# Idle matmuls from the first microseconds, the parameter rows spread at another place, and one batch's attention moved six steps ahead

## The chip, the cores and the metric

The kernel runs on one core of a Trainium2 chip. A core has five engines that work side by side, each through its own instructions in order: TensorE (PE) multiplies matrices into PSUM, VectorE (DVE), ScalarE (ACT) and GpSimd (POOL) work on elements, and SyncE (SP) mostly starts DMA transfers. They wait for each other through semaphores. The metric is the time of one execution on the device in microseconds, and the figure quoted is the median of several runs.

## The reference

Sliding-window attention with sink tokens is followed by a mixer block; each of the four batches is independent, only the parameters are shared.

```python
# q, k, v: (4, 8, 768, 64); n_sink = 4; window = 128
scores = scale * np.matmul(q, k.transpose(0, 1, 3, 2))
keep = (pos[None, :] < n_sink) | ((rel >= 0) & (rel < window))   # rel = query - key
a = softmax(np.where(keep, scores, -1e9))
x = np.matmul(a, v)                        # -> (4, 768, 512): heads side by side

a1 = alpha1 * x + beta1
u = x + lam * np.einsum('ts,bsd->btd', w_tok, a1)      # mixes the 768 tokens
a2 = alpha2 * u + beta2
out = u + lam * (np.maximum(a2 @ w_ch1, 0.0) @ w_ch2)  # 512 -> 2048 -> 512
```

Inputs and the output are float32; the kernel multiplies in fp16.

## The kernel before

Per batch, q and k are loaded, cast to fp16 (`n`, L317 and L315) and transposed into `qkT`: on TensorE for batches 0 and 1 (`tp`, L521), by DMA for batches 2 and 3 (L534). The 768 rows are six blocks of 128. For each key block j, `scores` (L607, L612) multiplies it with the queries of its own and the next block, which is all that the window reaches. ScalarE takes the exponential into `E` (L627). In batch 0, TensorE adds the mask before the exponential (L607); in later batches VectorE multiplies it in afterwards (L636). The sink keys have a small product of their own (`sk`, L560, with key slices `ks`, and `es`, L565). `pv` (L652, L659) multiplies with v, and VectorE divides by the sum (L682, L683). Batch 0 is done in two halves of four heads (G = 0, 1), so that its first half can start before all of q and k is there.

GpSimd then makes `xh` (L692, L701, L704): x times lam*alpha1, and plus lam*beta1 (in batch 0 this part is added in the token product instead, by a seventh matmul with the row sums of w_tok, L790; `lb` and `rsr` serve for it). `tok` (L786) is the token product, six output blocks per batch with six matmuls each; VectorE adds it to x (L795), which gives u. u is cast (`u16`), transposed to `uT` (on TensorE in batch 0, L830; by DMA later, L848) and scaled by alpha2, beta2 (L813, L815). `mlp1` (L869) makes 16 blocks of `h` for each of two chunks of three row blocks, with the relu on ScalarE or VectorE (L875, L877). `mlp2` (L893) multiplies with w2, which VectorE or GpSimd has multiplied with lam on its way to fp16 (`w2f`, L768), in four parts for each of six row blocks. VectorE adds (L904), and SyncE stores (L907).

The parameters come as rows. lam, alpha1 and beta1 are single rows of 512 elements. GpSimd multiplies two of them with lam (L938, L940). `spread` (L759) then copies a row to all 128 partitions by a float32 matmul of a column of ones with it: `b_la` for lam*alpha1, `b_lb1b` for lam*beta1, `b_lam` for lam. VectorE or ScalarE copies the result to `la_b`, `lb_b` and `lam_b`. alpha2 and beta2 are transposed into columns (`abT`, L949).

PSUM has eight banks. Four are homes of kind "d", taken by everything that TensorE makes except the scores; two homes of two banks each, kind "S", are for the scores.

The order of all this isn't written out. Every step is a task with a priority, costs in nanoseconds for each engine that may do it, the tasks that it follows and the buffers that it uses. `Plan.emit` runs a model of the engines and DMA rings once, when the program is made. It repeatedly picks the task that can start earliest (by priority among equals), gives it the engine and a home for its buffers, and writes its instruction at the end of that engine's queue. A change in one planned time can therefore reorder everything that follows, and even choose another engine for a step. On the chip, each engine goes through its queue in that order and waits as its data demands.

Where the model sees TensorE without work ahead of a task, up to 36 us of planned time (`IDLE`), it puts in idle matmuls: 128x128 products of the identity `iden` into a free home of kind "d" (L308) whose result nobody reads. Their number is the planned gap divided by 75 ns, counted from 900 ns at the earliest. The model counts TensorE's costs twice for tasks that start before 4500 ns.

Later batches are laid over earlier ones: while batch b is in mlp1 and mlp2, attention of batch b + 1 is spread over the same steps. Each batch's MLP is a list of steps with priorities w0, w0 + 1, and so on; the attention steps of the next batch get priorities that run evenly from w0 + lo to w0 + hi. For batch 1, lo is `LO`; for batches 2 and 3 it is 1. SyncE's queue holds loads, DMA transposes and stores in planned order; GpSimd's has casts, products and the issue of four loads of w1 (L480).

Of the kernel before, what the change touches and what calls it, by code (L numbers as in the profile page):

```python
# [15 lines left out]
PE, ACT, DVE, POOL, SP = "pe", "act", "dve", "pool", "sp"  # L16
# [91 lines left out]
class Plan:  # L108
# [10 lines left out]
    def add(self, prio, engs, fn, after=(), uses=(), mode=None, lands=None, port=False,  # L119
            since=0.0):  # L120


        t = Task(prio, engs, fn, after, uses, mode, lands, port)
        t.ready = max(t.ready, since)
        for b in uses:
            b.left += 1
        for a in t.needs:
            a.then.append(t)
        self.tasks.append(t)
        return t  # L130

    def emit(self):
        order = sorted(range(len(self.tasks)), key=lambda i: (self.tasks[i].prio, i))
        rank = {id(self.tasks[i]): r for r, i in enumerate(order)}
        waiting = {id(t): len(t.needs) for t in self.tasks}
        open_ = []
        free = {e: 0.0 for e in (PE, ACT, DVE, POOL, SP)}
        rings = Rings()

        def admit(t):  # L140
            bisect.insort(open_, (rank[id(t)], t), key=lambda x: x[0])

        def end(t, seen):
            t.seen = seen
            for b in t.uses:
                b.left -= 1
                b.freed = max(b.freed, seen)
                if b.left == 0:
                    self.busy[b.kind][b.home] = False
                    self.homes[b.kind][b.home] = b.freed  # L150
            for o in t.then:
                o.ready = max(o.ready, seen)
                waiting[id(o)] -= 1
                if not waiting[id(o)]:
                    admit(o)

        def pick():
            best = None
            for r, t in open_:
                at = t.ready  # L160
                for b in t.uses:
                    if b.t is None and b.home is None:
                        homes = [h for h, x in zip(self.homes[b.kind], self.busy[b.kind]) if not x]
                        n = sum(1 for o in t.uses if o.t is None and o.kind == b.kind)
                        if len(homes) < n:
                            at = None
                            break
                        at = max(at, sorted(homes)[n - 1])
                if at is None:
                    continue  # L170
                for e in t.engs:
                    at_e = max(free[e], at)
                    if e == POOL or (e == DVE and t.port):
                        at_e = max(at_e, port)
                    key = (at_e, r, at_e + t.engs[e])
                    if best is None or key < best[0]:
                        best = (key, t, e)
            return best

        for t in self.tasks:  # L180
            if not waiting[id(t)]:
                admit(t)
        mode = None
        port = 0.0
        landing = float("inf")
        done = 0
        while done < len(self.tasks):
            best = pick()
            if best is None or landing <= best[0][0]:
                assert landing < float("inf"), "no task can go on"  # L190
                t = rings.step(float("inf"))
                end(t, rings.now + 300.0)
                landing = rings.peek()
                continue
            (start, r, _), t, e = best
            open_.remove((r, t))
            for b in t.uses:
                if b.t is None:
                    spare = [i for i, x in enumerate(self.busy[b.kind]) if not x]
                    b.home = min(spare, key=lambda i: self.homes[b.kind][i])  # L200
                    self.busy[b.kind][b.home] = True
                    pool, shape, dtype = self.pools[b.kind]
                    b.t = pool.tile(b.shape or shape, b.dtype or dtype,
                                    tag=f"{b.kind}_{b.home}", bufs=1, name=b.name)
            until, idle, took = self.fill
            n = int((start - max(free[PE], 900.0)) / took)
            if e == PE and free[PE] < until and n > 0:
                free_d = [(h, i) for i, (h, x) in enumerate(zip(self.homes["d"], self.busy["d"])) if not x]
                if free_d and min(free_d)[0] < free[PE]:
                    h = min(free_d)[1]  # L210
                    idle(self.pools["d"][0].tile(
                        [P_, 512], FP32, tag=f"d_{h}", bufs=1, name=f"idle{done}"), n)
                    self.homes["d"][h] = start
                    mode = None
            t.fn(e)
            cost = t.engs[e]
            if t.lands:
                cost += rings.room("sw" if e == POOL else "hw", t.lands, start) - start
            if e == PE:
                if start < 4500.0:  # L220
                    cost = cost * 2
                if t.mode != mode:
                    cost = cost + 95
                mode = t.mode
            free[e] = start + cost
            if e == POOL or (e == DVE and t.port):
                port = free[e]
            t.at = (e, start, free[e])
            done += 1
            if t.lands:  # L230
                rings.step(start)
                rings.issue("sw" if e == POOL else "hw", t, free[e])
                landing = rings.peek()
            else:
                end(t, free[e] + SEEN[e])
        self.ends = free
# [3 lines left out]
def kernel(  # L240
# [72 lines left out]
    def copy(e, o, i):  # L313
        if e == ACT:
            nc.scalar.copy(o, i)  # L315
        else:
            engine[e].tensor_copy(o, i)  # L317
# [88 lines left out]
    w1f = const.tile([P, NC, DFF], FP16, name="w1f")  # L406
    w2f = const.tile([P, NF, DM], FP16, name="w2f")

    ROWS = 5500.0
    SPREAD = -790  # L410
    W1_SINCE = 20000.0

# [23 lines left out]
    def load_v(p, b, r, wait=None):  # L436
        bf = vn[b, r] = Buf("vnat", None, None, f"vnat{b}_{r}")
        done["vn", b, r] = add(
            p, {SP: 550}, lambda e: nc.sync.dma_start(
                bf.t, v[b, :, r * P : (r + 1) * P, :].rearrange("h p d -> p h d")),  # L440
            [wait], [bf], lands=(64, 19.0))
# [314 lines left out]
    def spread(p, name, src, o):  # L756

        pt = Buf("d", None, None, f"b_{name}")
        a = add(p, {PE: 900}, lambda e: nc.tensor.matmul(pt.t, ones_r, src, start=True, stop=True),  # L759
                [done.get(name)], [pt], since=ROWS)  # L760
        done[name] = add(p + 0.1, {DVE: 600, ACT: 600}, lambda e: copy(e, o, pt.t), [a], [pt])
# [153 lines left out]
    n = 0  # L915
# [21 lines left out]
    def spread_rows():  # L937
        done["la1"] = add(-880, {POOL: 1270}, lambda e: nc.gpsimd.tensor_mul(rows[1], rows[1], rows[0]),  # L938
                          since=ROWS)
        a = done["lb1b"] = add(-878, {POOL: 1270}, lambda e: nc.gpsimd.tensor_mul(rows[2], rows[2], rows[0]),  # L940
                               since=ROWS)
        z = add(-990, {POOL: 400}, lambda e: nc.gpsimd.memset(lb16.t, 0.0), [], [lb16])
# [6 lines left out]
        a = add(-850, {PE: 200}, lambda e: nc.tensor.transpose(pt.t, ab_row, iden8), [], [pt],  # L949
                since=ROWS)  # L950
        done["ab2"] = add(-800, {DVE: 100, ACT: 230}, lambda e: copy(e, ab2, pt.t), [a], [pt])
# [21 lines left out]


    STEP = 100.0
    LO = 12
    LEAD = 46.0
    for b in range(B):
        w0 = STEP * b
# [30 lines left out]
        if b + 1 < B:  # L1010
            nb = b + 1
            if nb >= XB:
                for i, (hp, t) in enumerate(QK_ORDER):
                    load_qk(w0 + i, nb, hp, t, done["qkT", b, 3, 1])
                for r in range(NR):
                    load_v(w0 + 10 + r, nb, r, done["qkT", b, 3, 1])
            lo, hi = (1, ns - 14) if b else (LO, ns - 12)
            steps = [("T", i) for i in range(8)] + [("sk",)]
# [58 lines left out]
```

## Time and profile before

| what | before |
|---|---|
| median of 6 runs | 272.58 us (271.46 to 274.88) |
| the profiled execution | 271.86 us, span 270.2 us |
| TensorE busy | 257.2 us, 95% of the span, 1844 matmuls |
| VectorE, ScalarE, GpSimd busy | 144.4, 134.8 and 109.5 us |
| HBM read and written | 29.63 and 6.29 MB |
| token products L786 | 34.5 us, 144 matmuls |
| mlp1 L869 | 90.2 us, 512 matmuls |
| mlp2 L893 | 89.0 us, 384 matmuls |

The span runs from the first to the last instruction of the program; what lies around it belongs to the execution's time too. [...] matmuls are pipelined, so the distance between two starts says how fast TensorE goes, not the length of one. In a line of the timeline, the bracket tells how long the engine was idle before it, and what ended that.

### The profile page before, as it was taken

The page shows a single profiled execution, that of the slowest core. Times are in us where ns is not written, and L with a number is a line of the kernel's source. Part 1 is how long each engine was busy: PE and PEld are TensorE (multiplying, and loading weights), DVE is VectorE, ACT ScalarE, POOL GpSimd, SP SyncE. Part 2 cuts the span into 40 slices and gives each one's busy share as a digit, 9 for nine tenths or more (in the row PEclk, how much of TensorE's full clock was granted, in tenths as well). Part 3 has the DMA queues.
Part 4 walks back from the last instruction along what each step waited for, and adds up shares of the span by engine and source line. Part 5 has one row for each costly group of instructions (what it writes and reads, how often), then busy time and mean ns, then how long its engine had stood idle before and what let it go on. Part 6 is the DMA issues. An engine that isn't in the chain of part 4 may idle for free.

```text
span 270.2 us, 4769 instructions
## 1 busy us (share of the span) xinstructions
PE 257.2 (95%) x1844; PEld 137.5 (51%) x1844; DVE 144.4 (53%) x299; ACT 134.8 (50%) x222; POOL 109.5 (41%) x124
## 2 busy tenths in 40 slices
PE   3899989998999999799999999999999999999994
PEld 2344555764554554356555444555654445665441
DVE  4267665579798755727894235378952344000222
ACT  3359983766756224878870024787600136773000
POOL 8544893667492672035595223005755000000000
PEclk9999999999999999999999999999999999999999
DMA  6999999929953999499919897200011252000222
GB/s 208 335 230 367 379 295 247 164 80 271 268 86 82 227 238 212 107 245 229 183 31 143 181 232 175 61 0 2 0 41 40 97 98 79 0 0 2 79 78 78
DMA packets 85484, 39.64 MB, mean 147 GB/s; under 512 B 73419, under 2 KB 79571, under 8 KB 85462
## 3 DMA queue, kind: packets, MB, share of 16 engines
q1 hardware_dynamic: 83328, 37.24, 55.9%
q0 software_dynamic: 2112, 2.10, 4.6%
q8 instruction: 14, 0.23, 0.4%
q14 instruction: 8, 0.07, 0.1%
q10 hardware_dynamic: 22, 0.01, 0.0%
HBM read 29.63 MB, written 6.29 MB: 133 GB/s over the span
## 4 chain that ended last, share of the span: by engine, by line
PE 89%; DVE 4%; DMA 3%; issue 1%; ACTq 0%; ACT 0%; SPq 0%; DVEq 0%
PE ch L893 31%; PE h L869 30%; PE tok L786 10%; PE S L612 4%; PE pv L659 4%; PE tp L521 2%; DMA ab_row<-in_moe_beta_dram 2%; DVE w2f L768 2%; PE S L607 2%; PE pv L652 1%; DMA qkT<-n 1%; PE b_lb1b L759 1%; PE b_la L759 1%; PE b_lam L759 1%; DVE qkT L317 1%; PE sk L560 1%
## 5 line engine op out<-in xcount | busy, mean ns | idle before, releaser
L869 PE MATMUL h<-uT,w1f 128*128 128x384 f16 x512 | 90.2, 327 | 0.8 <-DVE hT L877 0.7
L893 PE MATMUL ch<-w2f,hT 128*128 128x512 f16 x384 | 89.0, 379 | 0.0
L869 PEld LDWEIGHTS <-w1f 128*128 128x128 f16 x512 | 47.5, 98 | 32.8 <-issue 3.8
L893 PEld LDWEIGHTS <-hT 128*128 128x128 f16 x384 | 35.9, 98 | 40.4 <-issue 0.4
L875 ACT ACTIVATE hT<-h 128x384 f16<-128x384 f32 x90 | 44.1, 491 | 22.9 <-PE h L869 22.5
L627 ACT ACTIVATE E<-S 128x1024 f16<-128x1024 f32 (+1 forms) x42 | 40.6, 1003 | 9.5 <-PE S L612 5.4
L904 DVE TENSOR_TENSOR x<-x,ch 128x512 f32<-128x512 f32 x24 | 16.5, 686 | 49.7 <-PE ch L893 49.2
L701 POOL TENSOR_TENSOR tmp<-x,la_b 128x512 f32<-128x512 f32 x18 | 26.0, 1446 | 42.0 <-DVE x L683 39.6
L786 PE MATMUL tok<-xh,wtokT 128*128 128x512 f16 x144 | 34.5, 379 | 0.0
L315 ACT CAST u<-x 128x512 f16<-128x512 f32 x18 | 11.1, 618 | 43.0 <-DVE x L795 43.0
L877 DVE TENSOR_SCALAR hT<-h 128x384 f16<-128x384 f32 x38 | 20.9, 554 | 16.6 <-PE h L869 16.1
L795 DVE TENSOR_TENSOR x<-x,tok 128x512 f32<-128x512 f32 x24 | 16.5, 687 | 21.5 <-PE tok L786 16.6
L704 POOL TENSOR_TENSOR xh<-tmp,lb_b 128x512 f16<-128x512 f32 x18 | 24.6, 1365 | 1.3
L317 POOL CAST vf<-vnat 128x512 f16<-128x512 f32 x18 | 12.6, 705 | 27.5 <-DMA vnat<-in_v_dram 13.7
L636 DVE TENSOR_TENSOR E<-E,maskn 128x1024 f16<-128x1024 f16 x25 | 23.4, 966 | 0.0
L786 PEld LDWEIGHTS <-wtokT 128*128 128x128 f16 x144 | 13.9, 98 | 15.9
L683 DVE TENSOR_TENSOR x<-pv,rec 128x256 f32<-128x256 f32 x48 | 20.4, 424 | 1.7
L659 PEld LDWEIGHTS <-E 128*128 128x128 f16 x328 | 15.7, 98 | 6.1 <-issue 1.4
L659 PE MATMUL pv<-vf,E 128*128 128x65 f16 x328 | 18.3, 194 | 0.0
L317 POOL CAST n<-nat 128x768 f16<-128x768 f32 x15 | 12.7, 859 | 9.8 <-DMA nat<-in_k_dram 4.1
L612 PE MATMUL S<-qkT 64*128 64x256 f16 (+1 forms) x168 | 14.3, 280 | 1.9 <-DMA qkT<-n 1.9
L315 ACT CAST n<-nat 128x768 f16<-128x768 f32 x13 | 10.6, 832 | 9.0 <-DMA nat<-in_q_dram 6.6
(100 smaller groups left out, 203.1 us busy)
## 6 DMA issues: line engine op xcount, KB each, us to landing
nat<-in_q_dram SPq DMA_DIRECT2D x16, 384.0 KB, 6.2
nat<-in_k_dram SPq DMA_DIRECT2D x16, 384.0 KB, 3.7
out_dram<-x SPq DMA_DIRECT2D x24, 256.0 KB, 2.3
vnat<-in_v_dram SPq DMA_DIRECT2D x18, 256.0 KB, 4.5
wst_w<-in_moe_w_ch_dram SPq DMA_DIRECT2D x8, 512.0 KB, 9.6
wtn<-in_moe_w_tok_dram SPq DMA_DIRECT2D x6, 384.0 KB, 5.7
w1f<-in_moe_w_ch_dram POOLq DMA_DIRECT2D x4, 512.0 KB, 13.4
v<-in_v_dram SPq DMA_DIRECT2D x12, 128.0 KB, 5.1
```

The source lines that it names most:

```text
L315: nc.scalar.copy(o, i)
L317: engine[e].tensor_copy(o, i)
L612: nc.tensor.matmul(pv_[:, e_, i, :], o.t[rows, 2 * hp + 1, j * P : (j + 1) * P], o.t[rows, 2 * hp, j * P : j * P + w], start=not bias, sto ...
L627: nc.scalar.activation(eT.t, pS.t[:, :, 0 : n * w].rearrange("p e (i w) -> p e i w", i=n), AF.Exp, scale=scale)
L636: nc.vector.tensor_mul(ev, ev, m.to_broadcast(list(ev.shape)))
L659: nc.tensor.matmul(po.t[:, hl, :], eT.t[:, e_, off + i, c : c + P], vf[j][:, h, :], start=(r < 2 and n == 0), stop=(n == len(parts) - 1 an ...
L701: nc.gpsimd.tensor_mul(tmp.t, bx.t.rearrange("p h d -> p (h d)"), la1_b)
L704: nc.gpsimd.tensor_add(bh.t, tmp.t, lb1_b)
L786: nc.tensor.matmul(pt.t, wtokT[:, si, ti * P : (ti + 1) * P], hs[si].t, start=(si == 0), stop=(si == NR - 1 and b > 0))
L869: nc.tensor.matmul(ph.t, w1f[:, c, fi * P : (fi + 1) * P], bu.t[:, c, chk * NTOK : (chk + 1) * NTOK], start=(c == 0), stop=(c == NC - 1))
L875: nc.scalar.activation(bh.t[:, fi, :], ph.t, AF.Relu)
L893: nc.tensor.matmul(pc.t, bh.t[:, fi, nt * P : (nt + 1) * P], w2f[:, fi, :], start=(fi == 0), stop=(fi == NF - 1))
```

## The change

Two conditions of the idle matmuls in `Plan.emit` change. Before 4500 ns of planned time, their number is now the gap divided by 110 ns. A free home of kind "d" may now be taken also if it became free at exactly the moment when TensorE did, which includes moment zero, when nothing has run yet.

`ROWS`, the planned time before which the row products and spreads may not start, goes from 5500 to 7500 ns. `LO`, the place among batch 0's MLP steps at which batch 1's attention begins, goes from 12 to 6.

```diff
@@ -203,10 +203,10 @@
             until, idle, took = self.fill
-            n = int((start - max(free[PE], 900.0)) / took)
+            n = int((start - max(free[PE], 900.0)) / (took if free[PE] > 4500.0 else 110.0))
             if e == PE and free[PE] < until and n > 0:
                 free_d = [(h, i) for i, (h, x) in enumerate(zip(self.homes["d"], self.busy["d"])) if not x]
-                if free_d and min(free_d)[0] < free[PE]:
+                if free_d and min(free_d)[0] <= free[PE]:
                     h = min(free_d)[1]
@@ -406,7 +406,7 @@
-    ROWS = 5500.0
+    ROWS = 7500.0
     SPREAD = -790
     W1_SINCE = 20000.0
@@ -973,7 +973,7 @@
     STEP = 100.0
-    LO = 12
+    LO = 6
     LEAD = 46.0
     for b in range(B):
```

The program that this makes has 72 idle matmuls instead of 12, and nothing else is added or left out. Its queues differ from the old ones in these places, which the prediction speaks of:

- TensorE starts with 29 idle matmuls; 6, 14 and 5 more stand between the first transposes, and 3, 4, 10 and 1 later. Before, there were 6, 1, 3 and 2.
- TensorE's start was tp, tp, abT, b_lam, b_la, tp, vsp, tp, b_lb1b, S, S, sk. It is now tp, tp, tp, abT, tp, b_lam, vsp, b_la, S, S, sk, b_lb1b.
- On GpSimd the cast of the third tile stands ahead of the two row products instead of between them. `lam_b` and `lb` are made by ScalarE ahead of the first exponential instead of by VectorE; `la_b` goes the other way.
- One more qkT copy and two small `ks` copies lie among ScalarE's first exponentials, and one v cast fewer.
- GpSimd issues the four w1 loads earlier among its xh products.
- In batch 0's MLP, the first scores of batch 1 come five h blocks sooner, its first value product right behind `vsp` instead of six h blocks later; four w2f products follow each other on VectorE.
- vsp and the first scores of batch 2 stand behind ten or more h blocks of batch 1's MLP instead of ahead of the first. One part of mlp2 of batch 0 comes after the third token product of batch 1.

## The prediction

> **What bounds the kernel now.** I read the page's parts 1 and 4 first: TensorE is the bound.
>
> ```profile
> PE 257.2 (95%) x1844; PEld 137.5 (51%) x1844; DVE 144.4 (53%) x299; ACT 134.8 (50%) x222; POOL 109.5 (41%) x124
> ...
> PE 89%; DVE 4%; DMA 3%; issue 1%; ACTq 0%; ACT 0%; SPq 0%; DVEq 0%
> ```
>
> Busy is not useful, so I read TensorE's timeline from 0 to 50 us next (start, duration, line, tile, count):
>
> ```profile
> 5.28 0.84 PE L308 MATMUL idle<-iden 128*128 128x128 f16 x6
> 5.92 0.84 PE L521 MATMUL tp<-iden,n 128*128 128x128 f16 x6
> 7.69 0.24 PE L949 MATMUL abT<-iden,ab_row 8*128 8x8 f32 x1 [0.93 <-DMA ab_row<-in_moe_beta_dram]
> 7.81 2.04 PE L759 MATMUL b_lam<-row,ones_r 1*128 1x512 f32 x2
> ...
> 13.60 2.07 PE L759 MATMUL b_lb1b<-row,ones_r 1*128 1x512 f32 x2
> 15.60 1.04 PE L612 MATMUL S<-qkT 64*128 64x256 f16 x8
> ...
> 19.36 0.61 PE L612 MATMUL S<-qkT 64*128 64x256 f16 x4
> ...
> 21.23 0.39 PE L612 MATMUL S<-qkT 64*128 64x256 f16 x4
> ...
> 29.86 0.33 PE L308 MATMUL idle<-iden 128*128 128x128 f16 x3
> ```
>
> Six idle matmuls take 5.92 - 5.28 = 0.64 us, 107 ns each; three at 29.86 are followed at 30.02, 53 ns each. The same four score matmuls take 0.61 us at 19.36 and 0.39 at 21.23. So TensorE runs at half speed until about 21 us, though the page prints 9 for the clock from the start: the trace's first clock record, "full", is at 20.87 us. From 7.69 us on it has no gap, with three row spreads of 2 us each ahead of the first scores.
>
> ScalarE's timeline says what waits for that (in brackets: idle time before, and what ended it):
>
> ```profile
> 16.25 1.94 ACT L627 ACTIVATE E<-S 128x1024 f16<-128x1024 f32 x2 [1.31 <-PE S L612]
> 18.08 0.59 ACT L565 ACTIVATE es<-sk 64x512 f16<-64x512 f32 x1
> 20.01 1.02 ACT L627 ACTIVATE E<-S 128x1024 f16<-128x1024 f32 x1 [1.35 <-PE S L612]
> ...
> 28.78 1.94 ACT L627 ACTIVATE E<-S 128x1024 f16<-128x1024 f32 x2 [0.57 <-PE S L612]
> ...
> 31.43 1.51 ACT L627 ACTIVATE E<-S 128x1024 f16<-128x1024 f32 x2
> ```
>
> Batch 0's twelve exponentials run from 16.25 to 32.94 us and are the thread of this stage: ScalarE is busy 11.56 of 12.80 us between 20.9 and 33.7. After that, TensorE's starts follow each other at the streaming rate. Adding up the starts that come later than that, I find 2.0 us lost from 46.5 to 75.2, 0.4 to 100.2, 2.3 to 111 (one gap), 2.6 over the remaining 159. So whatever the start saves is carried to the end, unless a later wait takes it. The one gap:
>
> ```profile
> 100.25 7.93 PE L786 MATMUL tok<-xh,wtokT 128*128 128x512 f16 x36
> 108.02 0.38 PE L579 MATMUL vsp_None<-vf,sel 128*128 128x512 f16 x1
> 108.33 0.50 PE L612 MATMUL S<-qkT 64*128 64x256 f16 x6
> 110.73 0.28 PE L612 MATMUL S<-qkT 64*128 64x256 f16 x2 [1.90 <-DMA qkT<-n]
> ```
>
> [...] its two clock records (full at 20.87, half at 270.05, 3.8 us after the last matmul) stand 249.17 us apart[...]. [...] here 17.46 to 20.87 held about 1.7 us of transposes and still raised the clock, while 14.05 to 17.46, with 1.6 us of row spread, did not. [...] a w2f product on VectorE takes 0.68 us alone and up to 1.75 beside GpSimd. [...] 16 engines, which are full here (share 1.04 to 1.14 from 20.9 to 46.5).
>
> **The change, part by part.** The order of the changed program's instructions is known without running it.
>
> *Idle matmuls.* Now 29 ahead of the first transposes, then 6, 14, 5, later 3, 4, 10 and 1; 72 instead of 12. `iden` is ready when its select ends on GpSimd (1.08 + 0.30 = 1.38 us). 29 x 0.107 = 3.1 us ends at about 4.5; the first transposes wait for VectorE's cast, which ends at 3.97 + 0.64 = 4.61. Cost nothing, that wait hides it. With the transposes and the next 20, TensorE is dense from 1.45 to 7.4 or 8.1 us, [...] the clock comes up 12 to 16 us earlier. The later ten idle (10 x 0.055 = 0.55) stand before a transpose that waits for ScalarE's `wt` anyway; bounds 0 to 0.6, I take 0.
>
> *Rows at 7500.* On GpSimd the cast of the third tile (0.82, its data is there at 8.02) now precedes both row products (1.59 and 1.25): they end at 8.07 + 0.82 + 2.84 = 11.7. `tp_1_0` follows at 8.95, `tp_1_1` at 9.85 (VectorE's cast of the tile that lands at 9.2), its evacuation ends at 9.95 + 0.17 + 0.96 + waits = 11.3. The spreads cost half at full clock, 1.0 us each (a bound: 2.0 if cold): `b_lam` 10.2 to 11.2, `b_la` 11.3 to 12.3, first scores 12.3 to 12.8. `b_lb1b` goes behind the scores. ScalarE has `lam_b` (0.6), `ks` (0.4) and `lb` (0.6) first, done at 12.9. First exponential: 12.95 instead of 16.25, 3.3 us earlier.
>
> *The exponentials.* From first to last 32.94 - 16.25 = 16.7, of which 2.5 are waits for cold or backlogged TensorE (1.35 + 0.30 + 0.32 + 0.57). ScalarE gains one qkT copy (0.80) and `ks` (0.40) and loses one v cast (0.41). 16.7 - 2.5 + 0.8 = 15.0, plus 0.4 that I leave for waits: end at 28.35, 4.6 us earlier. Next in line would be GpSimd's `xh` products and the w_tok loads: the last of these lands at 28.2, its cast would be due at 37.7 - 4.6 = 33, so they do not bind. GpSimd's four w1f loads are issued up to 7 us earlier and share the full DMA engines; the sum of bytes stays, w1f arrives earlier, w2 and v rows up to 3 us later, and batch 1's v (53.9 us) is needed at about 60.
>
> *Batch 1's attention.* It moves work between slots that TensorE would fill anyway. Its first scores come five h blocks sooner, its first value product six, and four w2f products now stand in a row on VectorE ahead of three hT evacuations (before, two of these were in between). Before, three in a row took 3.82 us and cost TensorE 0.72. Four at 0.68 to 1.75 last 2.7 to 7.0; four PSUM homes cover about 2.6 to 4.0. Bounds -0.9 to +2.7; I take +0.3.
>
> *Batch 2's first scores* stand no longer ahead of its MLP. The MLP needs uT: from the end of the third token product VectorE 0.8, ScalarE 0.67, transpose issue to landing 2.35, affine 1.4, so 5.3 us. TensorE's cover is now three token products (3.9) and one channel part (0.86). 0.6 is lost, or 1.5 if SyncE is late by the 0.85 that it is now. Against 2.1 lost before: -0.9, bounds -1.5 to +0.4.
>
> Sum: -4.6 + 0.3 - 0.9 = -5.2 us. The profiled execution took 271.86 us (span 270.2 and 1.66 around it): 266.7. That execution is 0.7 below the median of 272.58. The six runs lie from 271.46 to 274.88, 3.4 apart[...]. I keep 266.7.
>
> **Rivals.** *The gain is eaten* (0.15): the clock rises, but VectorE's row of w2f (+2.7) or w2 and v landing 3 us later holds TensorE: 268.5 to 270.5. For: DMA is full until 46 us. Against: TensorE needs w2 only 20 us after it lands.
>
> *The idle work does nothing* (0.11): if the row spreads count as idle and the clock drops again behind them, the spreads take 2 us each, the first exponential is at 9.85 + 0.65 + 1.0 + 4 + ... = 16, as before. Left is -0.9 + 0.3: about 271.
>
> *Slower* (0.06): the clock falls back at about 11.7 and stays low longer than before, because `b_lb1b` now breaks the dense stretch later. [...] 6.8 us at half speed, cost 3.4 us: 271.9 + 3.4 = 275.3 and more. It decides from where the clock is still low at 26 us. Against: in the trace 2.1 us without a matmul (108.6) did not lower it.
>
> **Numbers.** The forecast's case, 263.8 to 268.5, has 0.68. The range leaves out the fastest corner and the slower rival with half of the second: 264.6 to 270.6. One per cent (2.7 us) is about what a measurement of this kernel can tell: faster 0.77 (0.68 and most of the eaten gain), within 0.16, slower 0.07.
>
> **What would show it.** Right: score matmuls at the fast spacing from the first, first exponential near 13 us, last ending near 28.4, batch 0's first `h` near 42, batch 2's first `h` with a gap below 1.5 us. Wrong: a late clock record, S before 20 us at 0.61, or a gap on `h` ended by VectorE's hT near 57 us of over 1.5 us.

## The result, and the profile after

The changed kernel takes 271.97 us (median of 32 runs, 269.66 to 274.10) against 272.77 us for the kernel before on the same chip (69 runs, 269.57 to 275.05): ratio 0.9977, 95% interval 0.9955 to 0.9999. That is 0.2%, where 1.9% had been predicted (266.7 us), and outside the predicted range. A ratio, here and below, is of fast runs alone (in each kernel without those more than 1.5% above its fastest), and it lies up to 0.4% from the quotient of the two medians. The profiled execution took 272.64 us, span 270.9.

The page of the changed kernel: busy times, the granted clock in forty slices of 6.8 us, and the shares of the chain that ended last.

```profile
PE 260.8 (96%) x1904; PEld 140.6 (52%) x1904; DVE 145.6 (54%) x299; ACT 133.5 (49%) x222; POOL 108.8 (40%) x124
...
PEclk9858999999999999999999999999999999999999
...
PE 92%; DMA 3%; DVE 2%; issue 1%; SPq 1%; ACT 0%; DVEq 0%; ACTq 0%
```

TensorE is the bound as before, and 3.6 us busier, no more than its 60 added idle matmuls. What to read is the clock row: 9, then 8 and 5, then 9 again. The trace's records say it exactly: full at 4.94 us, **half at 11.77**, full again at 22.01. Before, it came up once, at 20.87. TensorE's timeline of the changed kernel shows what that meant (start, duration, line, tile, count; in brackets the idle time before, and what ended it):

```profile
1.43 3.28 PE L308 MATMUL idle<-iden 128*128 128x128 f16 x29 [1.43 <-POOL iden L337]
4.67 0.62 PE L521 MATMUL tp<-iden,n 128*128 128x128 f16 x6
...
6.29 0.94 PE L308 MATMUL idle<-iden 128*128 128x128 f16 x14
9.16 0.51 PE L521 MATMUL tp<-iden,n 128*128 128x128 f16 x6 [1.93 <-POOL n L317]
9.51 0.44 PE L308 MATMUL idle<-iden 128*128 128x128 f16 x5
10.81 0.51 PE L521 MATMUL tp<-iden,n 128*128 128x128 f16 x6 [0.71 <-DVE n L317]
11.25 1.59 PE L759 MATMUL b_lam<-row,ones_r 1*128 1x512 f32 x2
...
13.09 2.07 PE L759 MATMUL b_la<-row,ones_r 1*128 1x512 f32 x2
15.09 1.03 PE L612 MATMUL S<-qkT 64*128 64x256 f16 x8
16.60 2.07 PE L759 MATMUL b_lb1b<-row,ones_r 1*128 1x512 f32 x2
...
20.21 0.61 PE L612 MATMUL S<-qkT 64*128 64x256 f16 x4
22.22 0.39 PE L612 MATMUL S<-qkT 64*128 64x256 f16 x4
```

The 29 idle matmuls end as the first cast is there. But from 7.23 us on TensorE stands still for 1.93 and then 0.71 us, waiting for casts, the clock falls in the middle of `b_lam`, and `b_la` and `b_lb1b` take 2.07 us each, as before. Score matmuls are at the slow 0.61 at 20.21 and reach 0.39 only at 22.22. ScalarE's timeline of the changed kernel:

```profile
15.74 1.94 ACT L627 ACTIVATE E<-S 128x1024 f16<-128x1024 f32 x2 [1.35 <-PE S L612]
...
20.86 1.02 ACT L627 ACTIVATE E<-S 128x1024 f16<-128x1024 f32 x1 [0.60 <-PE S L612]
22.65 1.02 ACT L627 ACTIVATE E<-S 128x1024 f16<-128x1024 f32 x1 [0.77 <-PE S L612]
...
32.87 1.50 ACT L627 ACTIVATE E<-S 128x1024 f16<-128x1024 f32 x2
```

Batch 0's exponentials begin at 15.74 (16.25 before) and end at 34.37 (32.94 before): the start lost 1.4 us instead of gaining 4.6. From there to the end of the span the kernel gained 0.7 back. In TensorE's timeline the one large gap of before, 2.06 us later than the streaming rate (that of matmuls without a wait between them), is now two smaller ones at the first `h` of batch 1's MLP (the prediction calls it batch 2's), 1.02 and 0.42 us:

```profile
105.38 4.05 PE L786 MATMUL tok<-xh,wtokT 128*128 128x512 f16 x18
110.28 0.61 PE L869 MATMUL h<-uT,w1f 128*128 128x384 f16 x2 [0.85 <-ACT uT L813]
111.15 2.11 PE L869 MATMUL h<-uT,w1f 128*128 128x384 f16 x12 [0.26 <-DVE uT L815]
```

### The profile page after: what moved, and what is told of

Read it like the earlier page. It is cut to its first block, busy times and chain, and to the rows that moved or that the text cites. A ratio compares the mean times of both kernels' runs of the same rounds, so it can differ in the third digit from the quotient of the medians.

```text
span 270.9 us, 4880 instructions
## 1 busy us (share of the span) xinstructions
PE 260.8 (96%) x1904; PEld 140.6 (52%) x1904; DVE 145.6 (54%) x299; ACT 133.5 (49%) x222; POOL 108.8 (40%) x124
## 4 chain that ended last, share of the span: by engine, by line
PE 92%; DMA 3%; DVE 2%; issue 1%; SPq 1%; ACT 0%; DVEq 0%; ACTq 0%
PE ch L893 31%; PE h L869 30%; PE tok L786 11%; PE S L612 5%; PE pv L659 4%; DMA nat<-in_k_dram 3%; PE tp L521 2%; PE S L607 2%; PE pv L652 2%; DVE E L636 1%; PE b_la L759 1%; PE b_lb1b L759 1%; PE sk L560 1%; PE wT L734 1%; PE b_lam L759 1%
## 5 line engine op out<-in xcount | busy, mean ns | idle before, releaser
L875 ACT ACTIVATE hT<-h 128x384 f16<-128x384 f32 x93 | 45.6, 491 | 21.3 <-PE h L869 21.1
L704 POOL TENSOR_TENSOR xh<-tmp,lb_b 128x512 f16<-128x512 f32 x18 | 25.5, 1415 | 1.3
L877 DVE TENSOR_SCALAR hT<-h 128x384 f16<-128x384 f32 x35 | 19.2, 553 | 10.9 <-PE h L869 10.5
L636 DVE TENSOR_TENSOR E<-E,maskn 128x1024 f16<-128x1024 f16 x25 | 24.2, 1000 | 0.0
L786 PEld LDWEIGHTS <-wtokT 128*128 128x128 f16 x144 | 13.8, 98 | 15.4
L317 POOL CAST n<-nat 128x768 f16<-128x768 f32 x17 | 14.0, 825 | 8.1 <-DMA nat<-in_q_dram 3.6
L317 POOL CAST u<-x 128x512 f16<-128x512 f32 x6 | 3.7, 622 | 27.2 <-DVE x L795 20.7
```

The source lines that it names most:

```text
L636: nc.vector.tensor_mul(ev, ev, m.to_broadcast(list(ev.shape)))
L704: nc.gpsimd.tensor_add(bh.t, tmp.t, lb1_b)
L786: nc.tensor.matmul(pt.t, wtokT[:, si, ti * P : (ti + 1) * P], hs[si].t, start=(si == 0), stop=(si == NR - 1 and b > 0))
L875: nc.scalar.activation(bh.t[:, fi, :], ph.t, AF.Relu)
```

## Does the clock decide the start?

Theory: the clock fell back because TensorE had too little to do around 7 to 12 us; keep it filled and the predicted gain appears. Rival: batch 0's attention is held by ScalarE, VectorE and the loads, whatever the clock. Three kernels with the changed kernel's order of instructions tell them apart; only the numbers of idle matmuls differ.

**No idle matmuls ahead of the first transposes and between them.** The first four groups are planned but not issued (`FORCE` gives the number that is issued, by group, counted from 0):

```diff
+FORCE = {0: 0, 1: 0, 2: 0, 3: 0}
...
-                        [P_, 512], FP32, tag=f"d_{h}", bufs=1, name=f"idle{done}"), n)
+                        [P_, 512], FP32, tag=f"d_{h}", bufs=1, name=f"idle{done}"), FORCE.get(self.idles, n))
+                    self.idles += 1
```

> The changed kernel, its order kept, without the first four groups of idle matmuls (54 of 72). Theory A: the clock comes up once only, at 19 to 25 us; the start runs cold, the first exponential comes at about 16.5 us instead of 15.7, and the time is 0.5 to 2 us above the changed kernel. Theory B: the time is that of the changed kernel within 0.5 us.

Measured: 273.52 us (20 runs), ratio 1.0068 (1.0048 to 1.0087). The clock came up at 23.55 us, the exponentials ran from 15.96 to 35.14. By the ratios that is 2.5 us above the changed kernel, a little over the band of theory A; the clock came up inside its band. So the new order without its early idle matmuls is a loss of 0.7%. The likely reason, an estimate, is that `b_lb1b` (2.07 us at half clock in the changed kernel), now behind the first scores, lies in the stretch from 16.7 to 20.1 that could have brought the clock up. The idle matmuls of the changed kernel did pay; they bought back what the order cost.

**A bridge and a filled gap.** The same edit, with more idle matmuls in the three groups between the transposes, and with 14 more ahead of each spread, written into the spread's own tile:

```diff
+FORCE = {1: 11, 2: 44, 3: 22}
...
+        def mm(e):
+            idle(pt.t, 14)
+            nc.tensor.matmul(pt.t, ones_r, src, start=True, stop=True)
```

> The changed kernel, its order kept, with more idle matmuls where TensorE waited: 11 instead of 6, 44 instead of 14, 22 instead of 5 among the first transposes, and 14 ahead of each of the three row spreads. Theory A (the clock fell back because TensorE was quiet from about 7 to 12 us): the clock stays up from the first window on, the first exponential comes at about 14.5 us, batch 0's exponentials end near 30 instead of 34.4, and the time is 3 to 4.5 us below the kernel before (267.5 to 269.5). Theory B (batch 0's attention is held by ScalarE, VectorE and loads in this order, whatever the clock): exponentials end at 33 or later and the time stays within 1 us of the kernel before.

Measured: 271.97 us (12 runs), ratio 0.9996 (0.9966 to 1.0026). The clock came up at 6.44 and stayed, as theory A had it, but the time is that of the rival. The groups of 14 stand in TensorE's way with about 0.87 us each, two of them ahead of the first scores and one behind; the exponentials began at 15.82 and ended at 32.42. A clock at full speed bought at that price was worth nothing here.

**The gap alone filled.** The same numbers, without the 14 ahead of each spread.

> As the bridge, without the idle matmuls ahead of the spreads. Theory A with spreads that count as idle: the clock falls one window later than in the changed kernel (about 15 us) and comes back after 18 us; first exponential near 13.5 us, exponentials end near 31.5, time 1.5 to 3 us below the kernel before. If spreads count as work: as the bridge or better, 3 to 5 us below. Theory B: no gain, within 1 us.

Measured: 270.29 us (20 runs), ratio 0.9931 (0.9903 to 0.9959); the profiled run took 268.11. TensorE's timeline of it:

```profile
6.67 2.62 PE L311 MATMUL idle<-iden 128*128 128x128 f16 x44
9.13 0.50 PE L524 MATMUL tp<-iden,n 128*128 128x128 f16 x6
9.46 1.39 PE L311 MATMUL idle<-iden 128*128 128x128 f16 x22
...
11.38 1.12 PE L762 MATMUL b_lam<-row,ones_r 1*128 1x512 f32 x2
...
12.65 1.12 PE L762 MATMUL b_la<-row,ones_r 1*128 1x512 f32 x2
13.70 0.61 PE L615 MATMUL S<-qkT 64*128 64x256 f16 x8
```

The spreads take 1.12 us instead of 2.07 and eight scores 0.61 instead of 1.03: the clock is full. The first exponential starts at 14.14 and the last ends at 29.85, so 4.5 us earlier than in the changed kernel, and all of it reaches the end of the span (266.4 against 270.9). The theory stands; the rival falls, since nothing that it names was touched.

The median gained less than that one run, 1.9 us by the ratio and so within the first band expected, because the clock stayed up in only three of the twenty runs. These have a mean granted clock of 0.998 or 0.999 and took 268.1 to 268.6 us. Seven runs at 0.994 took 269.1 to 269.9, and ten at 0.984 or 0.987 took 270.7 to 271.6: in those the clock fell after all. One and the same program thus went with its clock from a gain of 3.4 us over the kernel before (268.2 against 271.6) to one of 0.7. The next section shows why.

## What makes the clock fall

What this section says of the clock is read from the traces and runs of this case. The clock records of a trace lie on a grid of 3.413 us: in the changed kernel they are 6.83, 10.24 and 249.17 us apart, with the idle conditions alone 3.41, in the kernel before 249.17, which is 2, 3, 73, 1 and 73 times 3.413. The grid begins at different places: its first line lies 0.39 us behind the span's start in the kernel before, 0.88 with fp16 rows, 1.53 in the changed kernel, 3.24 with LO = 12 again. I laid it over every trace and added up, for each of its windows, TensorE's busy time (a single 128x128 matmul counts 0.22 us in it, six in a row 0.50): that of the spreads (L759), whose operands have a single row, and that of everything else, called wide here. "Full" and "half" are the speeds in the records, 1.0 and 0.5; four scores took 0.39 us at the one and 0.61 at the other. The windows in which something was decided (us):

| kernel | window | wide matmuls | row spreads | clock in it, behind it |
|---|---|---|---|---|
| changed | 4.94 to 8.36 | 1.97 | 0 | full, full |
| changed | 8.36 to 11.77 | 1.45 | 0.52 | full, **half** |
| LO = 12 again | 10.07 to 13.48 | 1.22 | 2.47 | full, **half** |
| idle conditions alone | 5.37 to 8.78 | 1.21 | 1.25 | full, **half** |
| fp16 rows | 7.70 to 11.12 | 1.69 | 0.41 | full, **half** |
| LO = 6 alone | 107.82 to 111.24 | 1.69 | 0 | full, **half** |
| gap filled | 13.02 to 16.44 | 1.75 | 1.87 | full, full |
| idle conditions alone | 107.77 to 111.18 | 1.86 | 0 | full, full |
| before | 109.62 to 113.03 | 2.30 | 0 | full, full |
| changed, rows at 5500 | 3.44 to 6.85 | 2.71 | 0 | half, half |
| fp16 rows | 0.88 to 4.29 | 2.85 | 0 | half, **full** |
| fp16 rows | 11.12 to 14.53 | 2.48 | 1.18 | half, half |

In the traces of this case a full clock fell exactly where a window held 1.69 us or less besides spreads, and never where it held 1.75 or more. Where between the two the border lies is not shown, and the ends of matmuls are modelled in a trace. A half clock rose behind 2.85 us or more of wide matmuls and not behind 2.71. The third row is the telling one: TensorE did not stand still at all in that window, the clock was full when it began, and the 2.47 us of single-row spreads did not save it. Spreads in fp16 did not count in full either: with them TensorE was busy for 1.94 us of the window from 7.70 and the clock fell, where 1.86 us of wide matmuls kept it; and the window from 11.12, with 2.48 us of wide matmuls and 1.18 of spreads, did not raise it.

The spread of the times goes with it. The changed kernel's runs fall into groups by mean clock: 269.7 to 271.0 us at 0.984 to 0.987, 271.2 to 272.7 at 0.978 to 0.981, 273.5 to 274.1 at 0.972 to 0.975. These are two, three and four windows at half speed (one window is half of 3.413 over 271, 0.006), some 1.8 us each. Which of them a run gets would then depend on where the grid lies; that is an estimate, which the fractions below bear out roughly. (Time ahead of a trace's first record counts as full in this mean: the kernel before has 1.000 in its trace, although it ran at half speed until 20.87. So a late rise does not show in it.) Of 63 runs of the kernel before on another chip, 33 had a mean of 0.992 to 0.994 and a median of 273.61 us, the other 30 a median of 271.81: one window more. On two more chips it was 17 of 27 and 12 of 47. Its long gap at 108.6 us is the only place that I find for it: in the profiled run it lay across two windows, which held 2.63 and 2.30 us, and so cost no clock, and two kernels of the next section with a like gap fell just there.

A grid laid at every offset over one trace gives an estimate of how often this should happen, with a fall behind every window of 1.71 us or less of wide matmuls (a value between 1.69 and 1.75). Behind the start, such a window turns up at 56% of the offsets for the kernel before (62 of its 137 runs have the lower mean) and at 27% for `LO` = 6 alone (9 of 22). In the start it turns up at 86% for the gap filled (17 of 20 runs below 0.998), at 26% for the bridge (2 of 12 at 0.993 or 0.994), and at none with the gap filled and the rows in fp16, below (none of ten runs at 0.994 or less). That is rough, since a fall moves what follows, but the order is right.

To test the gap at 108.6 us, I took the kernel before with `LO` = 6 alone, in which TensorE waits 1.68 us for uT ahead of batch 1's first `h`, and put idle matmuls into the free PSUM tile of that `h`:

```diff
         def mm(e):
+            if (b, chk, fi) == (1, 0, 0):
+                idle(ph.t, 20)
             for c in range(NC):
```

> The kernel before with LO = 6, and 20 idle matmuls (some 1.3 us) into the free tile of batch 1's first h, where TensorE had stood still for 1.7 us with the clock falling behind it for one stretch of 3.41 us. Theory (a stretch that is less than half full of wide matmuls lowers the clock for the next, about 1.8 us): the stretch around 108 us is now more than half full wherever it begins, no run shows a mean clock of 0.993 to 0.994 any more, and the median falls by 0.5 to 1 us against the same kernel without them (ratio to before 0.997 to 0.9995). Rival (the wait itself costs, the clock's fall is its companion): ratio unchanged at 1.001 to 1.003.

Measured: 272.32 us (22 runs), ratio 0.9993 (0.9965 to 1.0021), where the same kernel without them had 273.07 and 1.0017 (below; on another chip). The two intervals overlap, so the 0.75 us by itself is not shown. That the clock no longer falls there is: no run of 22 lies at 0.992 to 0.994, against 9 of 22 without the idle matmuls and 17 of 27 of the kernel before in the same comparison. And the two traces part the fall from the wait: from batch 0's first `h` to batch 1's, with the wait, both take 64.2 us; from there to batch 2's first `h` it is 59.18 us where the clock fell and 57.49 where it did not. One window at half speed cost 1.7 us there, beside the wait. TensorE's timeline, with the wait that is left:

```profile
108.61 0.38 PE L579 MATMUL vsp_None<-vf,sel 128*128 128x512 f16 x1
108.83 1.28 PE L308 MATMUL h<-iden 128*128 128x128 f16 x20
110.51 2.80 PE L871 MATMUL h<-uT,w1f 128*128 128x384 f16 x13 [0.40 <-DVE uT L815]
```

## What each part was worth

The change has three edits: the idle conditions, `ROWS` and `LO`. Here are three mixtures of them and `LO` alone, all on one chip. `ROWS` at 7500 beside the old idle conditions was not run.

The two idle conditions alone (against the changed kernel):

```diff
-    ROWS = 7500.0
+    ROWS = 5500.0
...
-    LO = 6
+    LO = 12
```

> Only the two conditions of the idle matmuls are changed; ROWS and LO stand as before, so that b_lam and b_la come right behind the third group of transposes with only one idle matmul between them. Theory A (the clock follows how full TensorE was in each stretch of about 3.4 us): the 29 idle matmuls bring the clock up at about 5 us, and it falls again within two such stretches, at 8.4 or 11.8 us, because b_lam and b_la stand where the stretch is empty; first exponential at 15.5 to 16.5 us, the last of batch 0's ends at 32 to 34.5, the time is that of before within 1 us (ratio 0.996 to 1.004). Rival (the rows' new place alone made the loss, and idle matmuls from the first microseconds are a pure gain): the clock stays up from 5 us, first exponential below 14.5 us, the time is 3 us or more below before (ratio below 0.99).

The same with `LO` = 6, that is, the changed kernel with `ROWS` put back:

```diff
-    ROWS = 7500.0
+    ROWS = 5500.0
```

> The changed kernel with the rows spread at their old place (ROWS 5500): against the kernel before it has the idle matmuls and LO = 6. If the shares add up: the time of the idle matmuls alone (first kernel of this set), less the 0.6 to 1.1 us that the later stages gain with LO = 6. If the rows' place at 7500 is what lost the start, this one is 3 us or more below the changed kernel (below 269); if the clock is, it lies within 1 us of the changed kernel (271 to 273).

`LO` = 6 alone (against the kernel before):

```diff
-    LO = 12
+    LO = 6
```

> The kernel before with LO = 6 alone: TensorE's first 200 matmuls stand in the old order, so the start is untouched (first exponential at 16.2, last of batch 0's ends at 32.9). If batch 1's place alone gives what the stages after 24 us gained in the changed kernel: 0.6 (the prediction's sum of -0.9 and +0.3) to 1.1 us (the trace's difference) below before, ratio 0.996 to 0.998, and TensorE waits less than 1.5 us at batch 2's first h. Rival (that gain came from the other order of the start, or from an idle stall put elsewhere): ratio 0.999 to 1.001, and the wait of 2.06 us at batch 2's first h is still there.

The changed kernel with `LO` put back:

```diff
-    LO = 6
+    LO = 12
```

> The changed kernel with LO = 12 again: the same question from the other side. If LO = 6 gave the later gain, this one is 0.6 to 1.1 us slower than the changed kernel (ratio to before 1.000 to 1.003), and the 2 us wait of TensorE at batch 2's first h is back; if not, it equals the changed kernel (0.996 to 0.999).

Measured, with the time that TensorE's starts lost to the streaming rate between 24 and 175 us in the profiled run:

| idle | ROWS | LO | median us (runs) | ratio to before, 95% | lost, us |
|---|---|---|---|---|---|
| old | 5500 | 12 | before | 1 | 9.3 |
| new | 5500 | 12 | 270.55 (8) | 0.9881 (0.9848 to 0.9915) | 9.5 |
| new | 5500 | 6 | 273.08 (20) | 0.9973 (0.9946 to 1.0000) | 11.7 |
| old | 5500 | 6 | 273.07 (22) | 1.0017 (0.9992 to 1.0043) | 11.6 |
| new | 7500 | 12 | 274.96 (22) | 1.0062 (1.0035 to 1.0089) | 10.8 |
| new | 7500 | 6 | 271.97 (32), the change | 0.9977 (0.9955 to 0.9999) | 8.1 |

I expected shares that add up. They do not. `LO` = 6 gave 0.85% with the rows at 7500, and with the rows at 5500 it cost 0.9% beside the new idle conditions, while 0.2% beside the old ones is within the noise; the rows at 7500 cost 1.8% with `LO` = 12 and nothing with `LO` = 6. The last column says through what: the plan is made anew each time, and the waits land elsewhere. With the rows at 5500 and `LO` = 6, TensorE waits between 66 and 77 us for a value product's PSUM home, and about 1.7 us for uT ahead of batch 1's first `h`; this is TensorE's timeline of the third kernel of the table, and the clock row of its page, with the fall behind that wait:

```profile
68.16 0.40 PE L659 MATMUL pv<-vf,E 128*128 128x65 f16 x8 [0.26 <-ACT hT L875]
69.50 0.82 PE L869 MATMUL h<-uT,w1f 128*128 128x384 f16 x4 [0.94 <-DVE x L683]
...
110.78 6.43 PE L869 MATMUL h<-uT,w1f 128*128 128x384 f16 x25 [1.52 <-DVE uT L815]
```

```profile
PEclk9999999999999999799999999999999999999999
```

So the rival for `LO` = 6 alone (the gain came from the order of the start) is nearer the truth than the theory, though the wait at the first `h` is neither under 1.5 us nor the old 2.06. The expectation for the last mixture had the right sign and was about three times too small, and the wait of 2 us did not come back at the first `h`: TensorE lost 1.84 us in the first token product, waiting for GpSimd's `xh`, and 1.1 at scores of batch 2, waiting for an exponential. In that kernel's profiled run the start was better than the changed kernel's (exponentials from 12.73 to 31.54), since the tile of the fourth group of transposes could be cast 1.3 us sooner and two spreads lay in full windows. Its 2.7 us come later, in the column "lost".

The idle conditions alone were the surprise: -1.2%, more than the whole change. Neither expectation holds: the clock did what the first theory said, and the ratio fell below the 0.99 of the rival. In the profiled run the clock came up at 5.37 and fell at 8.78, but `b_lam` lay in the full window (1.09 us instead of 2.04), and the old order brings the clock back at 19.02. The exponentials run from 14.76 to 31.27 and end 1.7 us earlier than before. The span gained 1.3; the median gained 2.2, and what goes beyond the span, 0.9 by the medians and more by the ratio, on eight runs, is not explained.

## Taking the cause away: rows in fp16

Behind the fall, a 1x512 fp32 spread, two matmuls in the timeline, takes 2.07 us, against 1.12 with the gap filled. With the rows in fp16 it is one matmul, of 0.38 to 0.60 us in the timeline below. The idle matmuls are those of the changed kernel:

```diff
-    ones_r = const.tile([1, P], FP32, name="ones_r")
+    ones_r = const.tile([1, P], FP16, name="ones_r")
+    row16 = [sb.tile([1, DM], FP16, tag=f"u16_{i}", bufs=1, name=f"rowh{i}") for i in range(3)]
+    nc.scalar.copy(row16[0], rows[0])
...
-        done["la1"] = add(-880, {POOL: 1270}, lambda e: nc.gpsimd.tensor_mul(rows[1], rows[1], rows[0]),
+        done["la1"] = add(-880, {POOL: 1270}, lambda e: nc.gpsimd.tensor_mul(row16[1], rows[1], rows[0]),
...
-        spread(-879, "la1", rows[1], la1_b)
...
+        spread(-879, "la1", row16[1], la1_b)
...
```

> The changed kernel with its idle matmuls as they are, and only the three spread rows and the vector of ones in fp16 (the products of the rows are rounded to fp16 ahead of the spread, the reference's fp32 is left). If it is the length of the fp32 spreads that gives the lost 4.6 us away, and the fall of the clock only through it: the clock may still fall at about 11.8 us, each spread takes 0.4 us warm and at most 0.8 cold, first exponential at 13 to 14 us, last of batch 0's ends at 30 to 31.5, time 269 to 270.5 (ratio 0.989 to 0.994). If the clock's fall holds the scores back whatever the spreads cost: first exponential above 14.5, time above 271 (ratio above 0.995).

Measured: 268.05 us (4 runs), ratio 0.9797 (0.9760 to 0.9835), below the expected band. TensorE's timeline:

```profile
10.56 0.38 PE L761 MATMUL b_lam<-rowh,ones_r 1*128 1x512 f16 x1
...
11.10 0.60 PE L761 MATMUL b_la<-rowh,ones_r 1*128 1x512 f16 x1
11.63 1.04 PE L614 MATMUL S<-qkT 64*128 64x256 f16 x8
...
13.14 0.60 PE L761 MATMUL b_lb1b<-rowh,ones_r 1*128 1x512 f16 x1
```

The clock fell at 11.12 here too (scores at 1.04) and was back at 17.94, yet the exponentials ran from 12.67 to 29.80. About 0.7 of the 3.1 us by which they begin earlier than in the changed kernel is not the edit's: in this run the cast of the tile for the fourth group of transposes could begin at 8.71 instead of 9.40, as its load landed sooner. Two of the four runs had such a fall by their mean clock, 0.987 (268.1 and 268.2 us), two had little or none, or a late rise (266.9 and 268.0). With the long spreads, three runs without a fall and ten at 0.984 or 0.987 lay some 2.7 us apart (the gap filled, above). So the fall by itself cost little here; with the long spreads behind it, it cost the start. Four runs carry this, and the rows in fp16 without the idle matmuls were not run.

The gap filled and the rows in fp16 (both edits above together):

> The gap filled as above, and the three rows spread in fp16 ([...] lam is cast by ScalarE at the start, the products are written as fp16, so lam, lam*alpha1 and lam*beta1 are rounded to fp16). Each spread should take 0.25 us instead of 1.0 warm or 2.0 cold. Theory A: the clock stays up or the spreads are too short to matter; first exponential near 13 us, exponentials end near 29.5, time 4 to 5.5 us below the kernel before. Theory B: within 1 us.

Measured: 267.72 us (4 runs), ratio 0.9852 (0.9788 to 0.9917), at the lower edge of theory A's band; the exponentials run from 13.66 to 28.71. Against the filled gap alone the start gained 1.1 us, and the profiled span nothing (266.7 against 266.4). The loss is in batch 0's MLP: from its first `h` to its first `ch`, the tile of mlp2, it takes 30.0 us, against 28.6. Timeline of this kernel, GpSimd, VectorE and TensorE:

```profile
54.13 2.10 POOL L320 CAST vf<-vnat 128x512 f16<-128x512 f32 x2
56.19 1.70 POOL L773 TENSOR_TENSOR w2f<-wst_w,lam_b 128x512 f16<-128x512 f32 x1
...
53.02 5.42 DVE L773 TENSOR_TENSOR w2f<-wst_w,lam_b 128x512 f16<-128x512 f32 x4
...
58.96 0.81 PE L874 MATMUL h<-uT,w1f 128*128 128x384 f16 x4 [1.32 <-DVE hT L882]
```

and VectorE's of the changed kernel, where the same four products met an idle GpSimd for most of their time:

```profile
58.68 2.73 DVE L768 TENSOR_TENSOR w2f<-wst_w,lam_b 128x512 f16<-128x512 f32 x4
61.39 1.86 DVE L877 TENSOR_SCALAR hT<-h 128x384 f16<-128x384 f32 x3
```

They take 0.68 us each there and 1.36 on average here, where GpSimd casts and multiplies at the same time. Four PSUM homes did not cover 5.42 us, and TensorE waited 1.32 us for the evacuation behind them.

The same with `LO` = 12:

> The gap filled and the rows in fp16, with batch 1's attention at its old place (LO = 12). If the place six steps ahead is worth what it was worth in the changed kernel (0.85%, 2.3 us, between LO = 6 and 12): 270 us, ratio 0.991 to 0.996. If the order of the start decides whether it helps (alone it gave nothing): 267 to 268.5, ratio 0.980 to 0.987, as with LO = 6.

Measured: 269.35 us (6 runs), ratio 0.9856 (0.9826 to 0.9886). The clock stayed up from 4.62; exponentials from 13.41 to 28.47. By the ratio the place is worth nothing here, by the traces (first `h` of batch 0 to that of batch 2: 122.3 us, against 120.9 with `LO` = 6) 1.4 us; between the two statements the runs do not decide. All three fp16 kernels beat both kernels of this case; which of them is best is open, with four to six runs each on two chips, on which the kernel before itself had medians of 271.61 and 273.11.

## Why the prediction was wrong, by its own steps

- *Idle matmuls.* "Cost nothing, that wait hides it" was right: 29 end at 4.71, the transposes start at 4.67. That "the clock comes up 12 to 16 us earlier", an estimate, was right too: 4.94 instead of 20.87. The step that failed is the unsaid one after it: that a clock which has come up **stays** up. In the window from 8.36 to 11.77 us TensorE had 1.45 us of wide matmuls, the clock fell at its end, and it was back only at 22.01. The step itself gave the end of the dense stretch (7.4 or 8.1; it was 7.23), and the next gave the next transposes as 8.95 and 9.85 (9.16 and 10.81). Between them lay the stretch that it never filled in, with little but two groups of transposes and five idle matmuls.
- *"In the trace 2.1 us without a matmul (108.6) did not lower it"* was the one reason against the fall. That gap happened to lie across two windows. By their mean clocks, 62 of 137 runs of that very kernel on three chips have one window more at half speed. One trace shows one position of the grid. Nor did a fall need a window without matmuls: every window here that began at full clock and had 1.69 of its 3.413 us or less in wide matmuls was followed by one. One window at half speed cost 1.7 to 1.8 us, half of the 3.4 between the prediction's six runs.
- *Rows at 7500.* "The spreads cost half at full clock, 1.0 us each (a bound: 2.0 if cold)": the bound came true for two of three. The first exponential came at 15.74, not 12.95. Of these 2.8 us, 1.6 are the clock (14.14 with the gap filled, where `tp_1_1` comes at 10.94, much as here). The other 1.2 are mostly the step's own: `tp_1_1` came at 10.81 instead of 9.85. The tile landed 0.2 us later than I had it, and VectorE's cast of it took 1.35 us instead of 0.65. The new order puts that cast beside GpSimd's product of a row; before, it stood apart. VectorE's and GpSimd's timelines of the changed kernel, and VectorE's of the kernel before:

```profile
9.40 1.35 DVE L317 CAST n<-nat 128x768 f16<-128x768 f32 x1 [3.51 <-DMA nat<-in_k_dram]
...
9.07 1.26 POOL L938 TENSOR_TENSOR row<-row,row 1x512 f32<-1x512 f32 x1
...
10.49 0.55 DVE L317 CAST n<-nat 128x768 f16<-128x768 f32 x1
```

In all eight traces with this order of the casts it took 1.34 to 1.40 us. (With the gap filled it ended at 10.25; there the 22 idle matmuls ahead of `tp_1_1` took the rest.)

- *The exponentials.* The 15.4 us from first to last (15.0 and 0.4 for waits), worked out for a TensorE at full clock, are 15.7 with the gap filled and 15.1 with `LO` = 12, the gap filled and fp16 rows; the end, predicted at 28.35, is 28.47 there. The step was right for the case that it assumed. In the changed kernel it was 18.6.
- *Batch 1's attention* (+0.3) and *batch 2's first scores* (-0.9), together -0.6: from the last exponential to the end of the span the changed kernel gained 0.7. That the sums agree is luck: from batch 0's first `h` to batch 2's it gained 1.4 (119.4 us against 120.8), and 0.7 were lost ahead of that, from the last exponential to the first `h` (14.3 against 13.5), which no step had. The four w2f took the low bound, 2.73 of "2.7 to 7.0", and cost nothing; with other timing they took 5.42 and cost 1.3. The gap at batch 1's first `h`: 1.44 us lost instead of 2.06, predicted 0.6 to 1.5. But these sizes hold for this one plan: with another start the same edit of `LO` is a loss.
- *Rivals.* The mechanism of "slower" is what happened, to the place ("falls back at about 11.7": 11.77), and its reason as well: `b_lb1b` breaks the dense stretch later, and without idle matmuls the clock comes up at 23.55. Its price was wrong: it put 6.8 us of half speed more than before; the clock was back at 22.01, 1.1 us later than before, and what happened ahead of the fall was left out. "The idle work does nothing" had the end about right (271), also through the clock dropping; it had a chance of 0.11. Together these two deserved more than 0.17: the prediction had worked out TensorE's holes from 7 to 11 us without adding up its busy time there.

## What to carry to other kernels

The idle matmuls that raised the clock paid only as far as what followed kept it up. In these traces a full clock stayed behind a window of 3.413 us with 1.75 us or more of wide matmuls and fell behind one with 1.69 or less. So look at TensorE's busy time without single-row matmuls in such windows, laid over the timeline at every offset, and fill those that hold too little, only where TensorE waits anyway. If a single-row fp32 matmul stands on the path, try it in fp16 first, where its rounding is allowed; added to the idle matmuls, that gave more here (1.8% by the ratios, four runs) than the idle matmuls had. In a kernel whose order a planner makes, measure an edit in the plan in which it will stand: what `LO` = 6 gave changed sign with its surroundings.

## What the runs showed of the hardware that I had not expected

- TensorE's clock fell without a pause. A window of 3.413 us with 1.22 us of wide matmuls and 2.47 of single-row fp32 ones, without a gap, lowered it; 1.75 beside 1.87 kept it. Single-row fp16 spreads did not count in full either: a window with 1.69 us of wide matmuls and 0.41 of them lowered it, where 1.86 of wide ones kept it.
- The groups of times of the changed kernel and of the kernel before, some 1.8 us apart, differ by windows at half clock, and the mean granted clock tells them apart (0.006 for each). It does not where the clock rises late: with the new idle conditions, rows at 5500 and `LO` = 6, runs at 0.975 and at 0.997 both took about 273.1 us.
- A 1x512 row spread takes 2.07 us in fp32 at half clock and 1.12 at full; in fp16 it takes 0.60 and 0.38.
- Beside a working GpSimd, four of VectorE's 128x512 `w2f` products took 1.36 us on average instead of 0.68, and its 128x768 cast 1.34 to 1.40 us instead of 0.55 to 0.64.
